# Attention with a gated MLP on one core: the query products, the output projection and the quotients are put in other places

## The chip, the cores and the metric

The kernel runs on one core of a Trainium2 chip. The core has a matrix engine (TensorE, PE in the profile; its weight loads are PEld), a vector engine (VectorE, DVE), a scalar engine (ScalarE, ACT), GpSimd (POOL) and a queue processor (SyncE, SP) from which nearly all DMAs of this kernel are issued. Each engine takes its own instructions in order and waits for others by semaphores. [...] The metric is the device time of one launch in microseconds. The kernel before takes 1242.56 us (median of three runs, 1242.16 to 1243.12).

## The reference

With x of 2048 tokens by 512 and 32 heads of width 128 over 2048 cached keys and values, all bf16:

```python
xn = layernorm(x)
q = (xn @ wq) per head                          # 32 heads of 128
p = softmax(q @ k_cache^T * 128**-0.5)          # 2048 x 2048 per head
s = concat_heads(p @ v_cache) @ wo              # 2048 x 512
h = gelu(layernorm(xn) @ w1)                    # four quarters, shifted by +1, -1, +2, -2 tokens
x1 = xn + shifted(h) @ w2
b = x1 + gelu(layernorm(x1) @ w3) @ w4          # w3: 512 x 1792
out = x + s * silu(b)
```

Nearly all of the work is the attention: scores, exponentials and weighted values for 32 heads.

## The kernel before, in words

The first 130 us or so compute the two normalisations and most of the MLP. Then comes one long loop over attention **units**. A unit is one head and one block of 512 query tokens: 8 groups of 4 heads, 4 query blocks per group, 4 heads, in that order, so 128 units, and four units in a row share their query block and head group. A unit has 8 **slots**, and a slot handles 256 keys: two score matmuls of 512 columns into a PSUM tile of two banks (`ps_s`, two such tiles), one exponential on ACT over 128x1024 into a bf16 tile (`pT`), and, ten slots later, two matmuls of these weights with the values (`ps_o`). The order of all instructions is written out by hand, slot by slot: each engine's program is the order in which the loop emits. Into the slots go further pieces, from here on called **extras** where they are TensorE's:

- **Query products.** The queries of two heads are made together by a seven-product scheme from xn (`xnT`, sums of it in `xs`) and the query weights (`wq_h`, sums and differences in `wc`), each product being two matmuls of 256 columns. For the pair with first unit v the products are spread over units v-2 (even) and v-1 (odd). Products 1, 6 and 2 are in the even unit, 7, 5, 4 and 3 in the odd one. They share one PSUM bank, tag `xa`: products 1 and 7 take a new tile of it. `q_take` (line 393, ACT) copies product 1 out (`tq`), and later the sum of products 1 and 2 (`qT`). `q_part` (lines 400 to 409, DVE) makes the other sums; its last step, line 407, frees the bank for the next pair.
- **Output projection.** When the four heads of a query block and group are done, four token tiles of 128 tokens are each multiplied with the four heads' `wo` rows: four matmuls of 512 columns per tile, one per chosen slot (`wo_slot`, list `at_wo`), into one PSUM bank (tag `xm`). The fifth step, `wo_post`, adds the tile's result to its fp32 sum (line 560, DVE). One tile is done per unit. In the last groups `wo_post` also plans scalings (lines 526 and 531) at slots counted from its own.
- **Softmax denominators.** DVE adds up the exponentials of a unit (lines 429, 434, 438, 442); a transposing DMA (`tT`) turns the result; DVE reduces it (`sm`, line 472) and takes the reciprocal (line 478). Through DRAM the reciprocals are written (`dr`) and read back as a broadcast to all partitions (`rb`). Two units later, in slot 7, `norm` (line 496, DVE) multiplies the unit's value result with `rb` into `oT`, the left side of the projection. Because of the transposing DMA, `rb` holds the tokens of the block in the order (p j), token j*128 + p. Before the change `oT` holds that order too, and the projection picks every fourth column.

DVE's program around the end of a unit reads: an addition of exponentials (slot 6), the projection's sum and the quotient (slot 7), the reduction, the reciprocal and another addition (slot 0 of the next unit). Units 14 to 123 follow the pattern that the change touches.

Of the kernel before, what the change touches and what calls it, by code (L numbers as in the profile page):

```python
# [17 lines left out]
def kernel(  # L18
# [26 lines left out]
    QT = Sq // 512  # L45
# [5 lines left out]
    HG = 4  # L51
# [77 lines left out]
    TURN = range(NU - HG)  # L129
# [185 lines left out]
    def q_mm(u, dcs, tag="xa"):  # L315
        g, qt, hh = units[u]
        if dcs[0] == 0:
            st[u] = dict(psq=psX.tile([P, 512], FP32, tag=tag, name="ps_q"))
        for dc in dcs:
            mm(st[u]["psq"][:], wqs[g * HG + hh][:, dc, :],  # L320
               xnT[:, dc, qt * 512:(qt + 1) * 512], dc == 0, dc == DC - 1)
# [73 lines left out]
    def q_part(v, i):  # L395
        s = sw[v]
        ps, t = s["ps"], lambda: pS.tile([P, 256], FP32, tag="tq", bufs=3, name="tq")
        if i == 0:
            s["u"] = t()
            pin(nc.vector.tensor_tensor(out=s["u"][:], in0=ps[:, 1, :], in1=s["m1"][:], op=ALU.add))  # L400
        elif i == 1:
            s["u3"] = t()
            pin(nc.vector.tensor_tensor(out=s["u3"][:], in0=ps[:, 0, :], in1=s["u"][:], op=ALU.add))
        elif i == 2:
            pin(nc.vector.tensor_tensor(out=s["q"][:, 3, :], in0=ps[:, 1, :], in1=s["u3"][:], op=ALU.add))
        else:
            pin(nc.vector.tensor_tensor(  # L407
                out=s["q"][:, 1:3, :], in0=ps[:], in1=s["u"][:].unsqueeze(1).to_broadcast([P, 2, 256]),
                op=ALU.add))
            del sw[v]  # L410

    def s_slot(u, p):
        g, qt, hh = units[u]
        s = st[u]
        sps = psS.tile([P, 2, 512], FP32, name="ps_s")
        for j in range(2):
            kc = 2 * p + j
            kv = kTs[g * HG + hh].rearrange("d (i p j) -> d i j p", p=P, j=KJ)
            mm(sps[:, j, :], kv[:, kc // KJ, kc % KJ, :], s["qT"][:], True, True)
        if p % 2 == 0:  # L420
            s.setdefault("pT", []).append(pB.tile([P, 4, 512], BF16, tag="pT", bufs=6, name="pT"))
        jj = 2 * (p % 2)
        pin(nc.scalar.activation(  # L423
            out=s["pT"][-1][:, jj:jj + 2, :], in_=sps[:], func=ACT.Exp, scale=SCALE))
# [7 lines left out]
    def add_next(u, i):  # L432
        a = st[u]["acc"]
        pin(nc.vector.tensor_tensor(out=a[:], in0=a[:], in1=st[u]["pT"][i][:], op=ALU.add))  # L434
# [34 lines left out]
    def turned_sums(u):  # L469
        s = st[u]  # L470
        sm = s["sm"] = smp.tile([P, 4], FP32, name="sm")
        pin(nc.vector.tensor_reduce(out=sm[:], in_=s["tT"][:], axis=mybir.AxisListType.X, op=ALU.add))  # L472

    def turned_recip(u):
        s = st[u]
        sm = s["sm"]
        rc = smp.tile([P, 4], FP32, name="rc")
        pin(nc.vector.reciprocal(out=rc[:], in_=sm[:]))
        s["dr"] = drp.tile([P, 4], FP32, name="dr")
        pin(nc.sync.dma_start(out=s["dr"][:], in_=rc[:]))  # L480

    def bcast(u):
        st[u]["rb"] = pB.tile([P, 512], FP32, tag="rb", bufs=2, name="rb")
        pin(nc.sync.dma_start(
            out=st[u]["rb"][:], in_=st[u]["dr"][:].rearrange("p j -> (p j)").partition_broadcast(P)))

    def norm(u):
        g, qt, hh = units[u]
        s = st.pop(u)
        if hh == 0:  # L490
            oTs[(g, qt)] = pB.tile([P, HG, 512], BF16, tag="oT", bufs=2, name="oT")
        o, rb, to = s["o"][:], s["rb"][:], oTs[(g, qt)][:, hh, :]
        if u in TURN:
            o = o.rearrange("k (j p) -> k p j", j=4)
            rb, to = (x.rearrange("k (p j) -> k p j", j=4) for x in (rb, to))
        pin(nc.vector.tensor_tensor(out=to, in0=o, in1=rb, op=ALU.mult))  # L496

    wo_box = {}
# [5 lines left out]

    def o_cols(g, qt, hh, ts):
        o = oTs[(g, qt)][:, hh, :]
        if (g * QT + qt) * HG + hh in TURN:
            return o.rearrange("k (p j) -> k j p", j=4)[:, ts, :]
        return o[:, ts * P:(ts + 1) * P]

    def wo_mm(g, t, hhs, tag="xm"):
# [28 lines left out]
    def pay():  # L540
        while owed:
            y_out(*owed.popleft(), nc.sync)
# [317 lines left out]
    def pv_run(n):  # L860
        while pv_at[0] <= n - LAG:
            pv_slot(*divmod(pv_at[0], SPU))
            pv_at[0] += 1
# [11 lines left out]
    def wo_slot(part, n, each=2, **kw):  # L875
        gg, t = wo_todo[0]
        if part < HG // each:
            wo_mm(gg, t, tuple(range(part * each, (part + 1) * each)), **kw)
            return
        wo_todo.popleft()  # L880
        wo_post(gg, t, n)
        if gg == NG - 1 and t % 4 < 3 and t + 1 not in fin and t // 4 not in LATE:
            fin_load(t + 1)
# [5 lines left out]
    first, third = {}, {}  # L889
    for v in pairs:  # L890
        a = (v - 2) * SPU
        for k, n in ((1, 1), (6, 2), (2, 5), (7, 8), (5, 9), (4, 12), (3, 13)):
            steps[a + n].append((product, v, k))
        for i, n in enumerate((1, 5)):
            steps[a + n].append((q_take, v, i))
        steps[a + 14].append((q_part, v, 3))
        first[v - 2] = v
        third[v - 1] = (v,)

    def fold_at(u):  # L900
        return 1 if u in third else 0

    def run_steps(n, which):
        for fn, v, k in steps.get(n, ()):
            if fn is which:
                fn(v, k)
# [4 lines left out]
    for h in range(HG, H, 2):  # L911
        u = (h // HG) * QT * HG + (-4, -2)[h % HG // 2]
# [8 lines left out]
    for n in range(UB * SPU):  # L921
        u, p = divmod(n, SPU)
        extra = len(wo_todo) > 1 and u in (2 * HG, 2 * HG + 1)
        if p == 0 and wo_box:
            wo_slot(4, n, each=1)
        s_slot(u, p)
        pv_run(n)
        for v, dcs in q_plan.get(n, ()):
            q_mm(v, dcs)
        run_steps(n, product)  # L930
        run_steps(n, q_take)
        if p == 0 and 1 <= u:
            if u - 2 in TURN:
                turned_sums(u - 2)
                turned_recip(u - 2)
            add_next(u - 1, 3)
        if p == 1 and u - 2 in TURN:
            bcast(u - 2)
        if p == fold_at(u) and 1 <= u:
            for v in third.get(u, ()):  # L940
                q_part(v, 1)
            fold(u - 1)
            for v in third.get(u, ()):
                q_part(v, 2)
            if u != UA and u not in first:
                fold_last(u - 1)
        if p == 2 and u in first:
            q_part(first[u], 0)
            fold_last(u - 1)
        if p == 3 and u - 1 in TURN:  # L950
            turn(u - 1)
        if p == 0:
            twice = extra
        if twice and p < 3:
            wo_slot(p, n, tag="xa")
        for v, k in ((u + 1, 3), (u + 2, 7)):
            if p == k and "psq" in st.get(v, ()) and (k == 3) == (v > FIRST):
                q_copy(v)
        if u - 2 in TURN:
            norm_p, sum_p, wo_p, each = 7, 5, 3, 1  # L960
        else:
            norm_p, sum_p, wo_p, each = 4, 5, 4, 1
        at_wo = [wo_p + i for i in range(HG // each + 1)]
        if FIRST - 2 <= u < LAST:
            at_wo = ([0, 3, 4, 6, 7], [0, 2, 3, 6, 7], [3, 4, 5, 6, 7], [0, 2, 3, 6, 7])[u % 4]
        if p == norm_p and 2 <= u and not u - 2 in TURN:
            norm_queue(u - 2)
        if p == sum_p and 1 <= u and u - 1 not in TURN:
            sums(u - 1)
        if p == sum_p + 1 and 1 <= u and u - 1 not in TURN:  # L970
            bcast(u - 1)
        if u == UA and p in (1, 2, 3):
            wo_slot(p - 1, n)
            if p == 3:
                fold_last(u - 1)
        if p in at_wo and wo_todo and pS is not None and (p == at_wo[0] or wo_box):
            wo_slot(at_wo.index(p), n, each=each)
        if p == norm_p and u - 2 in TURN:
            norm_queue(u - 2)
        run_steps(n, q_part)  # L980
        if p == 4:
            add_first(u)
        if p == 6:
            add_next(u, 2)
        pay()
        held_mm(n)
        for fn in todo.pop(n, ()):
            fn()
        if pS is None and not held:
            right.close()  # L990
            pS = right.enter_context(pool("pS", side="right", reuse_waits="tile"))
# [3 lines left out]
    n = UB * SPU  # L995
# [156 lines left out]
```

## Time and profile before

| | |
|---|---|
| median of three runs | 1242.56 us |
| profiled execution | 1240.9 us, its span 1239.1 us |
| TensorE, share of the span busy | 100% |
| ACT | 90% |
| DVE | 83% |
| DMA queue 1, share of 16 engines | 41.1% |
| granted TensorE clock | 1.0 |

The trace is of one execution. Engines' records give start, duration, line and the tiles written and read. Nearly every matmul is recorded under line 112, a helper, so matmuls are told apart by their tiles: `ps_s<-qT,kT` are scores, `ps_o<-pT,vb` weighted values, `ps_q` the query products, `ps_wo<-wo_h,oT` the output projection. Matmuls are pipelined and their ends are modelled, so a duration of 0.38 us for one of 512 columns is longer than the time from one start to the next. In the timeline, a row's first number is its start in microseconds from the start of the span, the second its duration, or that of the merged row where x2 or more stands at its end. In the chain of waits, each row is a piece of the chain that ended last. In the rows of groups, busy time and mean duration in ns stand behind the first bar, idle time before the group's instructions behind the second.

### The profile page before, as it was taken

What the parts mean: (1) busy time and instruction counts of PE and PEld (TensorE: products, weight loads), DVE (VectorE), ACT (ScalarE), POOL (GpSimd) and SP (SyncE); (2) the same over time, 40 slices, a digit from 0 to 9 for tenths busy, and PEclk for the clock granted to TensorE, in tenths of its full rate; (3) what the DMA queues carried; (4) which work ended last, traced back from release to release, by engine and by line L of the source; (5) the groups of instructions that cost most, each with busy time, mean ns of one, the idle gap of its engine ahead of it and who ended that gap; (6) DMA issues with size and microseconds to landing.
All of it is one profiled execution on the core that took longest, in us unless ns stands there. A gap on an engine that the chain in (4) does not pass through costs nothing.

```text
span 1239.1 us, 17537 instructions
## 1 busy us (share of the span) xinstructions
PE 1233.0 (100%) x6267; PEld 644.2 (52%) x6267; DVE 1030.3 (83%) x1647; ACT 1112.6 (90%) x1237; POOL 26.7 (2%) x75
## 2 busy tenths in 40 slices
PE   9999999999999999999999999999999999999998
PEld 6444444455555555555555555555555555555555
DVE  7712778898888888888889888888889999999997
ACT  6345999899999999999999999999999999999996
POOL 5300000000000000000000000000000000000000
PEclk9999999999999999999999999999999999999999
DMA  8760112554334423353243423443345435543332
GB/s 175 171 148 21 31 39 65 98 97 91 66 76 100 109 53 82 86 112 84 57 90 95 111 55 69 100 103 75 71 87 107 102 65 86 103 103 69 77 80 67
DMA packets 244056, 107.75 MB, mean 87 GB/s; under 512 B 194816, under 2 KB 227712, under 8 KB 243968
## 3 DMA queue, kind: packets, MB, share of 16 engines
q1 hardware_dynamic: 243408, 106.17, 41.1%
q8 instruction: 49, 0.80, 0.3%
q14 instruction: 39, 0.32, 0.1%
q10 hardware_dynamic: 560, 0.46, 0.1%
HBM read 67.50 MB, written 2.36 MB: 56 GB/s over the span
## 4 chain that ended last, share of the span: by engine, by line
PE 95%; DVE 3%; DMA 1%; ACT 1%; issue 0%; POOL 0%; DVEq 0%; ACTq 0%
PE ps_s L112 39%; PE ps_o L112 37%; PE ps_q L112 8%; PE ps_wo L112 8%; PE ps_m L112 2%; DVE acc L434 1%; ACT pT L423 1%; DMA rb<-dr 0%; DMA tT<-acc 0%; DVE sm L472 0%; DVE oT L496 0%; DMA xin<-in_A_x_dram 0%; PE ps_oh L112 0%; DMA dr<-rc 0%; DVE y L1014 0%
## 5 line engine op out<-in xcount | busy, mean ns | idle before, releaser
L423 ACT ACTIVATE pT<-ps_s 128x1024 bf16<-128x1024 f32 x1016 | 1019.8, 1025 | 54.4 <-PE ps_s L112 24.8
L112 PE MATMUL ps_s<-qT,kT 128*128 128x512 bf16 (+1 forms) x2064 | 609.0, 377 | 0.0
L112 PE MATMUL ps_o<-pT,vb 128*128 128x512 bf16 x1984 | 589.9, 379 | 0.0
L434 DVE TENSOR_TENSOR acc<-acc,pT 128x2048 bf16<-128x2048 bf16 x254 | 307.0, 1209 | 54.6 <-ACT pT L423 54.1
L112 PEld LDWEIGHTS <-kT 128*128 128x128 bf16 x2064 | 232.7, 113 | 147.4 <-issue 2.4
L112 PEld LDWEIGHTS <-vb 128*128 128x128 bf16 x1984 | 194.0, 98 | 216.9 <-issue 0.3
L429 DVE TENSOR_TENSOR acc<-pT 128x2048 bf16<-128x2048 bf16 x127 | 155.4, 1224 | 43.0 <-ACT pT L423 41.9
L112 PE MATMUL ps_wo<-wo_h,oT 128*128 128x512 bf16 x496 | 186.2, 379 | 0.0
L438 DVE TENSOR_TENSOR acc<-acc 128x1024 bf16<-128x1024 bf16 x127 | 87.4, 688 | 2.5
L496 DVE TENSOR_TENSOR oT<-ps_o,rb 128x512 bf16<-128x512 f32 x127 | 86.6, 682 | 1.5 <-DMA rb<-dr 1.2
L472 DVE TENSOR_REDUCE sm<-tT 128x4 f32<-128x512 bf16 x124 | 83.9, 677 | 2.0 <-DMA tT<-acc 2.0
L112 PEld LDWEIGHTS <-oT 128*128 128x128 bf16 x528 | 59.1, 112 | 49.5 <-issue 0.6
L112 PEld LDWEIGHTS <-wc 128*128 128x128 bf16 x440 | 42.9, 98 | 57.9 <-issue 12.7
L560 DVE TENSOR_TENSOR sacc<-ps_wo,sacc 128x512 f32<-128x512 f32 x96 | 65.7, 684 | 0.0
L112 PEld LDWEIGHTS <-wq_h 128*128 128x128 bf16 x398 | 38.9, 98 | 46.3
L112 PE MATMUL ps_q<-xnT,wq_h 128*128 128x256 bf16 (+1 forms) x288 | 61.1, 298 | 0.4 <-DVE sacc L548 0.4
L407 DVE TENSOR_TENSOR qT<-ps_q,tq 128x512 bf16<-128x512 f32 x55 | 38.0, 692 | 23.7 <-PE ps_q L112 23.5
L442 DVE TENSOR_TENSOR acc<-acc 128x512 bf16<-128x512 bf16 x127 | 53.0, 417 | 0.5
L293 ACT ACTIVATE h2T<-ps_s 128x1024 bf16<-128x1024 f32 x28 | 28.7, 1024 | 25.9 <-PE ps_s L112 25.9
L112 PEld LDWEIGHTS <-w_sb 128*128 128x128 bf16 x368 | 33.6, 98 | 29.6
L112 PE MATMUL ps_s<-xn2T,w_sb 128*128 128x512 bf16 x224 | 48.8, 379 | 0.0
L112 PE MATMUL ps_q<-xs,wc 128*128 128x256 bf16 x246 | 46.8, 271 | 0.0
(102 smaller groups left out, 586.4 us busy)
## 6 DMA issues: line engine op xcount, KB each, us to landing
rb<-dr SPq DMA_DIRECT2D x127, 256.0 KB, 3.9
vb<-in_A_v_cache_dram SPq DMA_DIRECT2D x62, 256.0 KB, 3.0
wq_h<-in_A_wq_dram SPq DMA_DIRECT2D x32, 128.0 KB, 3.1
wo_h<-in_A_wo_dram SPq DMA_DIRECT2D x32, 128.0 KB, 2.7
w_sb<-in_B_w_dram SPq DMA_DIRECT2D x8, 256.0 KB, 5.1
kT<-in_A_k_cache_dram SPq DMA_TRANSPOSE x128, 2.8
xl<-in_A_x_dram SPq DMA_DIRECT2D x16, 128.0 KB, 3.0
dr<-rc SPq DMA_DIRECT2D x127, 2.0 KB, 1.4
```

Of the source, the lines that this page charges most:

```text
L112: pin(nc.tensor.matmul(out=out, lhsT=lhsT, rhs=rhs, start=start, stop=stop, **kw))
L293: pin(nc.scalar.activation(out=h2[c, f][:], in_=ps[:], func=ACT.Gelu_apprx_tanh))
L407: pin(nc.vector.tensor_tensor(out=s["q"][:, 1:3, :], in0=ps[:], in1=s["u"][:].unsqueeze(1).to_broadcast([P, 2, 256]), op=ALU.add))
L423: pin(nc.scalar.activation(out=s["pT"][-1][:, jj:jj + 2, :], in_=sps[:], func=ACT.Exp, scale=SCALE))
L429: pin(nc.vector.tensor_tensor(out=s["acc"][:], in0=s["pT"][0][:], in1=s["pT"][1][:], op=ALU.add))
L434: pin(nc.vector.tensor_tensor(out=a[:], in0=a[:], in1=st[u]["pT"][i][:], op=ALU.add))
L438: pin(nc.vector.tensor_tensor(out=a[:, 0:2, :], in0=a[:, 0:2, :], in1=a[:, 2:4, :], op=ALU.add))
L442: pin(nc.vector.tensor_tensor(out=a[:, 0, :], in0=a[:, 0, :], in1=a[:, 1, :], op=ALU.add))
L472: pin(nc.vector.tensor_reduce(out=sm[:], in_=s["tT"][:], axis=mybir.AxisListType.X, op=ALU.add))
L496: pin(nc.vector.tensor_tensor(out=to, in0=o, in1=rb, op=ALU.mult))
L560: pin(nc.vector.tensor_tensor(out=sa, in0=ps[:], in1=sa, op=ALU.add))
```

## The change

- Product 1 of a query pair goes from slot 1 to slot 0 of its even unit, and so does the ACT copy of it.
- The four projection matmuls of a unit go to slots 3, 4, 6 and 7 of even units and 2, 3, 6 and 7 of odd ones. Before, the lists were 0, 3, 4, 6 (u%4 = 0), 0, 2, 3, 6 (odd) and 3, 4, 5, 6 (u%4 = 2), with the sum in slot 7.
- The lists have four entries now instead of five, so the sum is emitted by the rule at the top of the loop, `if p == 0 and wo_box`, at the head of the next unit, ahead of its first score matmuls. On DVE it so comes behind the quotient that slot 7 emits.
- The quotient (`norm`) walks the tokens in their own order: it reads PSUM and writes `oT` contiguously and reads `rb` at every fourth value. `o_cols` then picks 128 adjacent columns.

```diff
         if u in TURN:
-            o = o.rearrange("k (j p) -> k p j", j=4)
-            rb, to = (x.rearrange("k (p j) -> k p j", j=4) for x in (rb, to))
+            o, to = (x.rearrange("k (j p) -> k j p", j=4) for x in (o, to))
+            rb = rb.rearrange("k (p j) -> k j p", j=4)
         pin(nc.vector.tensor_tensor(out=to, in0=o, in1=rb, op=ALU.mult))
...
     def o_cols(g, qt, hh, ts):
         o = oTs[(g, qt)][:, hh, :]
-        if (g * QT + qt) * HG + hh in TURN:
-            return o.rearrange("k (p j) -> k j p", j=4)[:, ts, :]
         return o[:, ts * P:(ts + 1) * P]
...
-        for k, n in ((1, 1), (6, 2), (2, 5), (7, 8), (5, 9), (4, 12), (3, 13)):
+        for k, n in ((1, 0), (6, 2), (2, 5), (7, 8), (5, 9), (4, 12), (3, 13)):
             steps[a + n].append((product, v, k))
-        for i, n in enumerate((1, 5)):
+        for i, n in enumerate((0, 5)):
             steps[a + n].append((q_take, v, i))
...
         if FIRST - 2 <= u < LAST:
-            at_wo = ([0, 3, 4, 6, 7], [0, 2, 3, 6, 7], [3, 4, 5, 6, 7], [0, 2, 3, 6, 7])[u % 4]
+            at_wo = ([3, 4, 6, 7], [2, 3, 6, 7])[u % 2]
```

## The prediction

> **What bounds the kernel now.** I read the page first (busy time, chain of waits), then the chain in order of time, the busy time by stage and the row of one line, then the timeline of two places, last the groups and the waits. From the page:
>
> ```profile
> PE 1233.0 (100%) x6267; PEld 644.2 (52%) x6267; DVE 1030.3 (83%) x1647; ACT 1112.6 (90%) x1237; POOL 26.7 (2%) x75
> ...
> PE 95%; DVE 3%; DMA 1%; ACT 1%; issue 0%; POOL 0%; DVEq 0%; ACTq 0%
> ```
>
> TensorE carries 95% of the chain. A busy share of 100% doesn't say that it runs at its pace, so I compare pace with need. One row of the chain gives the pace, the row of line 393 (the copy of product 1, one per query pair) the real time, and the stage between its first and last start the busy times (PE, PEld, DVE, ACT, POOL, clock):
>
> ```profile
> 69.80 12.09 PE ps_o L112 x56
> ```
>
> ```profile
> L393 ACT ACTIVATE tq<-ps_q x55: 377/402/416, 249.1 to 1177.4; 128x256 f32<-128x256 f32 x55
> ```
>
> ```profile
> 249.10:1177.40 928.30, 927.65 (x4645) 486.44 (x4644) 821.18 (x1286) 888.24 (x974) 0.00 (x0) 1.00 0.42 86
> ```
>
> 56 matmuls of 512 columns take 12.09 us, 0.2159 us each. 54 pairs take 928.3 us, 17.19 each. A pair needs 2 x 16 score and 2 x 16 value matmuls, 8 of the output projection, and 7 products, each two matmuls of 256 columns, which I count as one of 512: 79 x 0.2159 = 17.06 us. The difference is 0.13 us, over 54 pairs 7 us. That is all that a better order of the same matmuls can win in this stage. The clock is 1.00. DVE idles 928.3 - 821.2 = 107 us, 0.99 us per unit (108 units), which is the cover for anything that DVE does more.
>
> Where the 0.13 us goes is seen at the slot after product 1. First a unit with u%4 = 0, TensorE and then ACT:
>
> ```profile
> 609.23 0.38 PE L112 MATMUL ps_q<-xnT,wq_h 128*128 128x256 bf16 x2
> 609.45 0.59 PE L112 MATMUL ps_s<-qT,kT 128*128 128x512 bf16 x2
> 609.88 0.59 PE L112 MATMUL ps_o<-pT,vb 128*128 128x512 bf16 x2
> 610.35 0.27 PE L112 MATMUL ps_q<-xs,wc 128*128 128x256 bf16 x1
> ```
>
> ```profile
> 609.92 0.38 ACT L393 ACTIVATE tq<-ps_q 128x256 f32<-128x256 f32 x1
> 610.18 1.03 ACT L423 ACTIVATE pT<-ps_s 128x1024 bf16<-128x1024 f32 x1
> ```
>
> Then one with u%4 = 2:
>
> ```profile
> 624.39 0.59 PE L112 MATMUL ps_s<-qT,kT 128*128 128x512 bf16 x2
> 624.82 0.59 PE L112 MATMUL ps_o<-pT,vb 128*128 128x512 bf16 x2
> 625.25 0.59 PE L112 MATMUL ps_s<-qT,kT 128*128 128x512 bf16 x2
> 625.68 0.59 PE L112 MATMUL ps_o<-pT,vb 128*128 128x512 bf16 x2
> 626.12 0.38 PE L112 MATMUL ps_q<-xnT,wq_h 128*128 128x256 bf16 x2
> 626.33 0.59 PE L112 MATMUL ps_s<-qT,kT 128*128 128x512 bf16 x2
> 626.76 0.59 PE L112 MATMUL ps_o<-pT,vb 128*128 128x512 bf16 x2
> 627.34 0.38 PE L112 MATMUL ps_q<-xs,wc 128*128 128x256 bf16 x2
> ```
>
> ```profile
> 624.16 2.86 ACT L423 ACTIVATE pT<-ps_s 128x1024 bf16<-128x1024 f32 x3
> 626.89 0.40 ACT L393 ACTIVATE tq<-ps_q 128x256 f32<-128x256 f32 x1
> ```
>
> Product 6 (ps_q from xs and wc) should start 2 x 0.216 us after the value matmuls: at 610.31 and 627.19. It starts at 610.35 and 627.34, 0.04 and 0.15 us late. Both times that is 0.05 us after the copy has ended (609.92 + 0.38 = 610.30; 626.89 + 0.40 = 627.29): product 6 writes the bank that the copy reads, and waits for it. The second place is worse because slot 0 there holds no extra matmul: the score matmuls of slots 0 and 1 come 0.86 us apart (624.39, 625.25). ACT needs more: three exponentials in 2.86 us, the last 1.03 us long, are a start every 0.92 us. ACT falls behind and takes the copy later.
>
> **The change, part by part.** The sum stands against the profiled execution (1240.9 us with what lies around its span); the median of the runs, 1242.56, is 1.7 us higher, and I take the same difference off it.
>
> *Product 1 and its copy one slot earlier.* Nothing is added; two matmuls and one copy move. On the first place's clock, slot 0 then has product 1 at 609.23 and the copy done at 610.30, as slot 1 has now. Slot 1 is left without an extra. Product 6 follows 0.22 (product 1) + 2 x 0.86 us (slot 1, and slot 2's score and value matmuls) after 609.23: 611.17, which is 0.82 us after the bank is free. The stall goes: the mean of 0.04 and 0.15 times 55 pairs, 5.2 us, under the ceiling of 7. What is late next: the exponential of slot 1 starts behind the copy at 610.18 and ends at 611.21; with 0.05 us of release its bank is free at 611.26, and the score matmuls of slot 3 want it at 611.17 + 0.22 = 611.39. The cover is 0.13 us: cost 0, but thin (a rival). Product 1 must also wait for the last addition of the pair before (line 407), which frees the bank. DVE, and TensorE's product 4:
>
> ```profile
> 619.60 0.42 DVE L405 TENSOR_TENSOR qT<-ps_q,tq 128x256 bf16<-128x256 f32 x1
> ...
> 622.65 0.69 DVE L407 TENSOR_TENSOR qT<-ps_q,tq 128x512 bf16<-128x512 f32 x1 [0.53 <-PE ps_q L112]
> 623.25 1.22 DVE L434 TENSOR_TENSOR acc<-acc,pT 128x2048 bf16<-128x2048 bf16 x1
> 624.39 0.68 DVE L560 TENSOR_TENSOR sacc<-ps_wo,sacc 128x512 f32<-128x512 f32 x1
> 624.99 0.68 DVE L496 TENSOR_TENSOR oT<-ps_o,rb 128x512 bf16<-128x512 f32 x1
> ```
>
> ```profile
> 621.15 0.38 PE L112 MATMUL ps_q<-xnT,wc 128*128 128x256 bf16 x2
> ```
>
> Line 407 ends at 623.34; product 1 would come 0.86 us into the slot that starts at 624.39, at 625.25: 1.9 us of cover, cost 0. For the first pair, line 327's query copy of slot 111 frees the bank; it stands on DVE where line 560 stands here, ends near 625.07 on this clock and is covered too, once.
>
> *The output projection in fixed slots.* Four matmuls per unit as before. Even units now have one extra in slots 0 and 2 to 7, odd units one in each; before, slot 7 was empty, odd slot 0 and one even slot 5 double. TensorE's sum is the same. The gain is counted already: with slots 7 and 0 filled ACT isn't behind when product 1 comes.
>
> *Sums at the unit's head.* The sum (line 560) changes place with the quotient (line 496) on DVE: the quotient at 624.39, the sum at 624.99. The matmul that it adds starts 0.86 us into slot 7, which began 0.86 us before 624.39, so at about 624.39, and ends 0.38 us later: no wait, and the reduction and reciprocal behind both keep their time. The bank is free at 625.67; the next tile's first matmul comes two slots and 0.86 us after 624.39, near 627.4. The quotient asks for its broadcast 0.6 us sooner; what it waits, DVE's idle time takes. Cost 0.
>
> *Scaling in the late groups.* Line 526 is queued from the sum's slot. In odd units it falls behind line 405, no longer ahead of it. Chain, then waits:
>
> ```profile
> 963.13 0.60 DVE sacc L526
> ...
> 965.05 0.38 PE ps_q L112 x2
> ```
>
> ```profile
> PE ps_q L112 <- DVE qT L405: 0.6, 2, 0.4
> ```
>
> At 965.05 the chain passes from DVE into product 4, with this 0.60 us in it. Out of the way, it ends these two waits, 0.6 us in all if the second is alike: gain 0.6.
>
> *Quotients in token order.* The operation reads PSUM contiguously instead of every 128th value, the broadcast at every 4th fp32 instead of contiguously, and writes contiguously as before; the projection's weight load, with a step until now, becomes contiguous.
>
> ```profile
> L112 PEld LDWEIGHTS <-kT 128*128 128x128 bf16 x2064 | 232.7, 113 | 147.4 <-issue 2.4
> L112 PEld LDWEIGHTS <-vb 128*128 128x128 bf16 x1984 | 194.0, 98 | 216.9 <-issue 0.3
> ...
> L496 DVE TENSOR_TENSOR oT<-ps_o,rb 128x512 bf16<-128x512 f32 x127 | 86.6, 682 | 1.5 <-DMA rb<-dr 1.2 <-PE ps_o L112 0.3
> ...
> L560 DVE TENSOR_TENSOR sacc<-ps_wo,sacc 128x512 f32<-128x512 f32 x96 | 65.7, 684 | 0.0
> ```
>
> A weight load with a step (kT) takes 113 ns, one without (vb) 98; either ends inside the 216 ns of the matmul before: gain 0. The quotient: a step in PSUM costs nothing (682 against 684 ns for the contiguous sum). No DVE row reads SBUF with a step; the nearest row is that weight load, 15% dearer, which would make 0.78 us. Bounds: 0.67 us (a gain too small to matter) to twice the 0.60 us between 624.39 and 624.99, 1.20. I take 0.68, the same engine's row. Up to about 0.9 us more would cost TensorE nothing: DVE has 0.99 us idle per unit, and product 4 at 621.15 stands 1.13 us behind the end of line 405 (620.02).
>
> [...]
>
> The sum: -5.2 - 0.6 = -5.8 us, from 1242.56 to 1236.8 (profiled: 1240.9 to 1235.1).
>
> **Rivals.** (1) The exponential takes product 6's place as the wait: if the 0.13 us of cover is overdrawn by 0.05 to 0.1 us, each of 55 pairs loses that, 2.8 to 5.5 us, and the kernel ends at 1239.6 to 1242.3. For it: ACT is busy 888.24 of 928.30 us. Against: it can start every 0.92 us, in slots of 1.08. (2) The quotient doubles to 1.20 us. DVE spends 0.6 of its 0.99 us; late broadcasts then reach TensorE now and then, and I allow up to half of the gain: 1237 to 1240, still faster. (3) The slower side: the read with a step takes so long that DVE becomes the bound. This decides from about 1.6 us per quotient (0.60 + 0.99); at three times the price, 1.8 us, DVE lacks 0.2 us in 108 units, 22 us, and the end is near 1259. For it: no row prices this read. Against: the step of 512 bytes in PSUM is free. (4) The change doesn't do what it says: product 6 waits for something that moves with it. Then 1242. Against: it starts 0.05 us after the copy's end in both places.
>
> **How the numbers follow.** A measurement of this kernel tells 0.2% (2.5 us) from no change. Forecast 0.58 and rival 2 0.14 are faster; rival 1 0.08 and rival 4 0.04 within; rival 3, to which I add what else may delay DVE, 0.16. So faster 0.72, same 0.12, slower 0.16. The range starts at 1235.0, where nearly all of the 7 us and the 0.6 are won, and ends at 1242.0, which leaves out little but rival 3. The forecast's own range is 1235.0 to 1239.0.
>
> **What would show it.** Right: the copies of product 1 near 17.08 us per pair apart instead of 17.19; product 6 directly behind the value matmuls; TensorE's wait for line 405 gone; line 496 near 680 ns, the oT weight load near 98. Wrong: line 496 above 1.2 us with TensorE waiting for DVE, score matmuls late in slot 3 of even units, or pairs still 17.19 us apart.

## The result: 1.6% slower, and the profile after

The changed kernel takes 1261.44 us (median of four runs, 1260.29 to 1265.34) against 1242.36 us for the kernel before beside it. The ratio is 1.016, 95% interval 1.0136 to 1.0183. I had forecast 1236.8. The profiled execution took 1260.29 us, its span 1258.5.

The page of the changed kernel: busy time, the chain of waits by engine and by line, two groups.

```profile
PE 1233.7 (98%) x6267; PEld 636.8 (51%) x6267; DVE 1077.8 (86%) x1647; ACT 1112.1 (88%) x1237; POOL 26.6 (2%) x75
...
PE 60%; DVE 19%; DMA 18%; issue 1%; ACT 1%; SPq 1%; DVEq 0%; ACTq 0%
PE ps_s L112 25%; PE ps_o L112 23%; DMA rb<-dr 10%; DMA dr<-rc 5%; PE ps_q L112 5%; PE ps_wo L112 5%; DVE oT L496 4%; DVE acc L434 4%; DMA tT<-acc 2%; DVE sm L472 2%; PE ps_m L112 2%; DVE sacc L558 2%; DVE acc L429 1%; DVE acc L438 1%; ACT pT L423 1%
...
L496 DVE TENSOR_TENSOR oT<-ps_o,rb 128x512 bf16<-128x512 f32 x127 | 135.5, 1067 | 33.1 <-DMA rb<-dr 31.4
...
L112 PEld LDWEIGHTS <-oT 128*128 128x128 bf16 x528 | 51.4, 98 | 59.1 <-issue 1.3
```

TensorE's busy time is the same, but it carries 60% of the chain instead of 95%. In its place stand DVE and two DMAs, the reciprocals' way out to DRAM (`dr<-rc`) and back as a broadcast (`rb<-dr`). The quotient of line 496 takes 1.07 us instead of 0.68. The list of waits of the changed kernel (total us, times, longest):

```profile
DVE oT L496 <- DMA rb<-dr: 31.4, 50, 2.4
...
PE ps_q L112 <- DVE qT L405: 17.3, 18, 2.1
```

50 quotients now wait for their broadcast, where 2 did, and TensorE waits 17.3 us for line 405, where it waited 0.6. (The projection's sum, line 560 before, has line 558 here.)

What the change does to product 6 came as forecast. TensorE's timeline of the changed kernel, product 1 in slot 0 and product 6 in slot 2:

```profile
611.56 0.38 PE L112 MATMUL ps_q<-xnT,wq_h 128*128 128x256 bf16 x2
...
613.07 0.59 PE L112 MATMUL ps_o<-pT,vb 128*128 128x512 bf16 x2
613.50 0.38 PE L112 MATMUL ps_q<-xs,wc 128*128 128x256 bf16 x2
613.72 0.59 PE L112 MATMUL ps_s<-qT,kT 128*128 128x512 bf16 x2
```

Product 6 starts 0.43 us, two matmuls, after the value matmuls, without the 0.04 or 0.15 us of delay. Yet the copies of product 1 are further apart:

```profile
L393 ACT ACTIVATE tq<-ps_q x55: 377/381/390, 248.8 to 1191.0; 128x256 f32<-128x256 f32 x55
```

942.2 us for 54 pairs is 17.45 us per pair, against 17.19 before: 13.9 us lost in this stage. Another 5.8 us lie behind it: from the last copy to the end of the span 67.5 us, 61.7 before.

The loss isn't spread evenly. By the starts of the single copies, 36 of the 54 pairs take 17.06 or 17.07 us in the changed kernel, the need of the prediction. The first 46 pairs together take 792.5 us against 790.3 before, the last eight 149.7 against 138.0. So of the 19.4 us by which the span grows, 17.5 fall into the last eight pairs and what follows them. From here on the **late groups** are the projections of the last group and of half the one before: there the sum is two operations (lines 551 and 554), or further ones come behind it (lines 567 and 569). One stretch there, before and then after (busy times of PE, PEld, DVE, ACT, POOL with the instructions, clock, DMA share, GB/s):

```profile
1060.00:1170.00 110.00, 109.60 (x550) 57.51 (x549) 102.91 (x163) 104.77 (x116) 0.00 (x0) 1.00 0.44 89
```

```profile
1060.00:1170.00 110.00, 101.72 (x508) 52.20 (x506) 100.19 (x153) 96.69 (x106) 0.00 (x0) 1.00 0.47 84
```

TensorE starts 508 matmuls there instead of 550, and DVE, although its quotients are dearer, is busy less than before. A DVE that is short of time doesn't look like that.

**Where the time went.** DVE around a unit's head in the changed kernel, in a part that runs without a stall:

```profile
610.48 1.08 DVE L496 TENSOR_TENSOR oT<-ps_o,rb 128x512 bf16<-128x512 f32 x1
611.48 0.68 DVE L558 TENSOR_TENSOR sacc<-ps_wo,sacc 128x512 f32<-128x512 f32 x1
612.08 0.67 DVE L472 TENSOR_REDUCE sm<-tT 128x4 f32<-128x512 bf16 x1
612.78 0.18 DVE L478 RECIPROCAL rc<-sm 128x4 f32<-128x4 f32 x1
```

From the quotient's start to the next reciprocal's start it is 2.30 us. Before, it was 1.30 (624.99 to 626.29). Now the same stretch in the chain of waits, in the late groups:

```profile
1076.35 1.00 DVE oT L496
...
1141.30 1.09 DVE oT L496
1142.38 0.61 DVE tm L551
...
1143.02 0.69 DVE sacc L554
1143.71 0.61 DVE sm L472
...
1144.34 0.19 DVE rc L478
...
1144.54 2.86 DMA dr<-rc
...
1147.42 3.28 DMA rb<-dr
...
1150.72 1.07 DVE oT L496
...
1159.98 1.08 DVE oT L496
```

This chain closes: the reciprocal starts the DMAs, the broadcast releases the quotient, and because DVE works in order (before the quotient at 1141.30 it sits idle for 1.10 us, until the broadcast has landed), the next unit's reduction and reciprocal stand behind that quotient. One turn per unit. The turn shown takes 9.42 us (1141.30 to 1150.72), the nine from 1076.35 to 1159.98 take 9.29 on average, and TensorE's unit is half of 17.06, 8.53. So in the late groups the units run at the pace of this chain, and DVE's additions and line 405, which product 4 waits for, come late.

That the chain is near its limit could be seen in the kernel before. Its timeline at a unit's head, and two rows of the DMA issues (the last number is the median time to landing):

```profile
626.29 0.18 DVE L478 RECIPROCAL rc<-sm 128x4 f32<-128x4 f32 x1
...
626.50 0.34 SPq L480 DMA_DIRECT2D dr<-rc  x1
...
628.94 0.34 SPq L484 DMA_DIRECT2D rb<-dr  x1
```

```profile
rb<-dr SPq DMA_DIRECT2D x127, 256.0 KB, 3.9
...
dr<-rc SPq DMA_DIRECT2D x127, 2.0 KB, 1.4
```

2.65 us from the reciprocal to the broadcast's issue, 3.9 to its landing, 1.30 on DVE: 7.85 us, 0.7 below 8.53. The change adds 0.4 (quotient) and 0.6 (the sum, now between quotient and reduction), which makes 8.85. But the way out varies: 2.44 us here, 2.86 in the chain above, 1.4 in the median. With the median a turn is about 1.0 us shorter, some 6.8 before and 7.8 after, and fits. In the late groups the sum is two operations, so 0.7 more, and there a turn no longer fits: of the nine above, eight are longer than 8.53. In the changed kernel the broadcast also lands later, 4.3 us in the median instead of 3.9; the runs don't show why.

### The profile page after: what moved, and what is told of

Same layout as the page of the kernel before. It is cut to its first block, busy times and chain, and to the rows that moved or that the text cites. A ratio compares the mean times of both kernels' runs of the same rounds, so it can differ in the third digit from the quotient of the medians.

```text
span 1258.5 us, 17538 instructions
## 1 busy us (share of the span) xinstructions
PE 1233.7 (98%) x6267; PEld 636.8 (51%) x6267; DVE 1077.8 (86%) x1647; ACT 1112.1 (88%) x1237; POOL 26.6 (2%) x75
## 4 chain that ended last, share of the span: by engine, by line
PE 60%; DVE 19%; DMA 18%; issue 1%; ACT 1%; SPq 1%; DVEq 0%; ACTq 0%
PE ps_s L112 25%; PE ps_o L112 23%; DMA rb<-dr 10%; DMA dr<-rc 5%; PE ps_q L112 5%; PE ps_wo L112 5%; DVE oT L496 4%; DVE acc L434 4%; DMA tT<-acc 2%; DVE sm L472 2%; PE ps_m L112 2%; DVE sacc L558 2%; DVE acc L429 1%; DVE acc L438 1%; ACT pT L423 1%
## 5 line engine op out<-in xcount | busy, mean ns | idle before, releaser
L496 DVE TENSOR_TENSOR oT<-ps_o,rb 128x512 bf16<-128x512 f32 x127 | 135.5, 1067 | 33.1 <-DMA rb<-dr 31.4
L112 PEld LDWEIGHTS <-oT 128*128 128x128 bf16 x528 | 51.4, 98 | 59.1 <-issue 1.3
L112 PE MATMUL ps_q<-xnT,wc 128*128 128x256 bf16 x194 | 37.0, 272 | 17.4 <-DVE qT L405 17.3
```

Of the source, the lines that this page charges most:

```text
L112: pin(nc.tensor.matmul(out=out, lhsT=lhsT, rhs=rhs, start=start, stop=stop, **kw))
```

## The experiments

The times are medians, each with the kernel before on the same chip and the ratio's 95% interval. The three theories are named in the first expectation: the chain (there called loop), DVE's load (occupancy), the sum's place as such.

**The quotient as before** (`e1_old_quotient`): the changed kernel with both edits of the quotient undone.

```diff
-            o, to = (x.rearrange("k (j p) -> k j p", j=4) for x in (o, to))
-            rb = rb.rearrange("k (p j) -> k j p", j=4)
+            o = o.rearrange("k (j p) -> k p j", j=4)
+            rb, to = (x.rearrange("k (p j) -> k p j", j=4) for x in (rb, to))
...
+        if (g * QT + qt) * HG + hh in TURN:
+            return o.rearrange("k (p j) -> k j p", j=4)[:, ts, :]
```

> The changed kernel with the quotient in its old order (PSUM read with a step, broadcast contiguous) and the old column picking; slots, product 1 and the sum's place stay changed. Three theories. Loop: the chain reciprocal, DMA out, DMA back, quotient, what stands on DVE up to the next reciprocal closes once per unit and must fit into TensorE's 8.53 us; in the changed kernel DVE's part of it is 2.31 us (3.04 to 3.50 in the late groups) against 1.31 before. Here it falls by 0.4 to 1.91, still 0.6 above before: most stalls go, some in the late groups stay; 1237 to 1244 us. Occupancy: only the 0.4 us more DVE work per quotient matters: all of the loss goes, 1236 to 1238 us. Place: the sum at the unit's head is what hurts: about 1258 to 1261 us.

1240.86 us, before 1240.58: ratio 1.0001 (0.9992 to 1.0011). With 0.39 us less per quotient the 1.6% are gone, but of what the slots should gain nothing is left over. That is inside the chain's range and above the one of occupancy.

**The quotient alone** (`e2_quotient_only`): the kernel before with the same two edits the other way round.

> The kernel before with only the quotient in token order; everything else as before. Loop: DVE's part grows from 1.31 to 1.71 us, in the late groups too, since the sum stands ahead of the quotient; product 6 still waits for the copy: 1242 to 1248 us. Occupancy: the whole of the extra DVE work is here, so at least the loss of the changed kernel: 1261 us or more. Place: nothing moves: 1242 us. In any case line 496 takes about 1.08 us and the oT weight load 98 ns.

1246.89 us, before 1240.58: 1.0049 (1.0034 to 1.0064).

```profile
L496 DVE TENSOR_TENSOR oT<-ps_o,rb 128x512 bf16<-128x512 f32 x127 | 134.9, 1062 | 3.5 <-DMA rb<-dr 3.1
```

The same dear quotient, the same extra DVE work as in the changed kernel, and 6 us of loss instead of 19. Occupancy as I had put it can't give that; neither is it nothing. On this run's page DVE is busy 90% or more in every slice from 1060 to 1170 us, so how much of the 6 us is the longer chain and how much is DVE's load stays open.

**The sum behind the next reciprocal** (`e3_sum_behind_recip`): the changed kernel, same operations, one of them later in DVE's order.

```diff
-        if p == 0 and wo_box:
+        if p == 0 and wo_box and not FIRST - 2 < u <= LAST:
             wo_slot(4, n, each=1)
...
                 turned_recip(u - 2)
+            if wo_box and FIRST - 2 < u <= LAST:
+                wo_slot(4, n, each=1)
```

> The changed kernel with the projection's sum emitted behind the next reciprocal instead of behind the quotient; the same operations of the same length on DVE, so the same DVE work. Loop: DVE's part of it falls from 2.31 to about 1.71 us and is no longer longer in the late groups; 1236 to 1241 us. Occupancy: same work, so no change: 1260 us. Place: the sum is still at the unit's head, 0.8 us later: 1260 us or more.

1241.71 us, before 1240.58: 1.0008 (0.9999 to 1.0017). With the same DVE work, 1.5% come back by taking 0.6 us (1.3 in late groups) out of the closed chain. That decides against occupancy and against the sum's place at the head as such. The time lies 0.7 us above the range that I had given for the chain.

**Both** (`e4_old_quotient_sum_behind`): the edits of the first and the third.

> Both: the old quotient and the sum behind the reciprocal; slots and product 1 as in the changed kernel. Loop: DVE's part is 1.31 us as before the change, and the gain that the slots should bring is left alone: 1236 to 1238 us, pairs 17.08 us apart. Occupancy: the same as e1_old_quotient. Place: about 1260 us.

1236.84 us, before 1240.58: 0.9971 (0.996 to 0.9982). Its rows: the spacing of the copies, and three waits.

```profile
L393 ACT ACTIVATE tq<-ps_q x55: 378/381/392, 248.5 to 1172.8; 128x256 f32<-128x256 f32 x55
```

```profile
DVE sm L472 <- DMA tT<-acc: 4.2, 7, 1.1
DVE oT L496 <- DMA rb<-dr: 2.3, 4, 1.2
...
PE ps_q L112 <- DVE qT L405: 1.5, 4, 0.9
```

17.12 us per pair, against 17.06 of need: the slots and product 1 do bring most of what they should, 3.7 us of the 5.8 forecast, once the chain has its old length. Beside this kernel the dear quotient costs 0.4% (e3), the sum between quotient and reduction 0.3% (e1), and both together 1.9%: the parts don't add up. That fits a chain that costs only what it exceeds TensorE's unit by. What the dear quotient costs alone may be DVE's load instead: in `e3` DVE is busy 106.45 of the 110 us from 1060 to 1170.

**Quotient and sum behind the reciprocal**, token order kept (`e5_quotient_behind_recip`) and with the old quotient (`e6_old_quotient_behind_recip`). To `e3` comes, for units 14 to 123:

```diff
                 turned_recip(u - 2)
+            if FIRST - 2 < u <= LAST:
+                norm_queue(u - 3)
...
-        if p == norm_p and u - 2 in TURN:
+        if p == norm_p and u - 2 in TURN and not FIRST - 2 <= u < LAST:
             norm_queue(u - 2)
```

> The changed kernel, token order kept, with the quotient of unit u-2 and the projection's sum both emitted behind the next unit's reciprocal. DVE does the same operations of the same length. Loop: the next reciprocal no longer stands behind the quotient, so a late broadcast can't delay it within one unit; the chain closes only over two units and has 17 us. 1236 to 1239 us, the wait of the quotient for its broadcast nearly gone, although the quotient still takes 1.08 us. Occupancy: 1260 us as the changed kernel.

> The same with the old quotient of 0.68 us. Loop: open and with 0.4 us less DVE work ahead of line 405; at or below e4_old_quotient_sum_behind, 1235 to 1237 us. Occupancy: 1236 to 1238 us, with all the difference to e5 (24 us) from the quotient's length.

1250.91 us, 1.0085 (1.007 to 1.01), and 1239.95 us, 0.9995 (0.9985 to 1.0004), before 1240.82. Both lie outside what either theory gave. Row and wait of the first:

```profile
L496 DVE TENSOR_TENSOR oT<-ps_o,rb 128x512 bf16<-128x512 f32 x127 | 132.5, 1043 | 0.3 <-PE ps_o L112 0.3
```

```profile
DVE sm L472 <- DMA tT<-acc: 18.9, 23, 1.9
```

The wait for the broadcast is gone, as the open chain wants it. But the reduction now waits 18.9 us for the transposing DMA (2.4 in the changed kernel, 4.2 in e4); with the old quotient, in `e6`, it waits 12.8. That DMA stands behind the last fold (line 442), the fold behind the additions, these behind the reciprocal: a second chain that closes once per unit, and quotient and sum had been put into it. How much of the loss is this chain and how much the dense DVE of the late groups, these runs don't separate.

**The step on the write** (`e7_step_on_write`): `e3` with the quotient in token order, the broadcast read contiguously and `oT` written with a step.

```diff
-            o, to = (x.rearrange("k (j p) -> k j p", j=4) for x in (o, to))
-            rb = rb.rearrange("k (p j) -> k j p", j=4)
+            o, to = (x.rearrange("k (j p) -> k p j", j=4) for x in (o, to))
+            rb = rb.rearrange("k (p j) -> k p j", j=4)
```

> e3_sum_behind_recip with the quotient in token order by a step on its write: it reads PSUM with a step as before, the broadcast contiguously, and writes every 128th bf16 of oT, 256 bytes apart. If the 0.4 us belongs to reading SBUF with a step alone, line 496 takes 0.68 us and the time is that of e4_old_quotient_sum_behind, 1236 to 1238 us, with the oT weight load at 98 ns. If any step in SBUF costs, about 1.08 us and 1241 us, as e3.

1311.98 us, 1.0575 (1.056 to 1.0591). Neither of the two cases: the write with a step is far dearer than the read.

```profile
L496 DVE TENSOR_TENSOR oT<-ps_o,rb 128x512 bf16<-128x512 f32 x127 | 304.9, 2401 | 7.1 <-DMA rb<-dr 6.4
```

```profile
DVE 62%; PE 20%; DMA 9%; issue 6%; ACT 1%; DVEq 0%; SPq 0%; ACTq 0%
```

At 2.4 us per quotient, 1.7 more than the old one, DVE carries 62% of the chain of waits and is busy 91% of the span. Here DVE itself may be the bound, as my third rival had it; but the closed chain is longer by the same 1.7 us, and this run doesn't separate the two.

**The chain made longer with no work added** (`e9_late_broadcast`): `e4` with the broadcast issued behind the transposing DMA.

```diff
-        if p == 1 and u - 2 in TURN:
+        if p == 1 and u - 2 in TURN and not 16 <= u < LAST:
             bcast(u - 2)
...
             turn(u - 1)
+            if 16 <= u < LAST:
+                bcast(u - 2)
```

> e4_old_quotient_sum_behind with the broadcast of units 16 to 123 issued behind the transposing DMA on the DMA queue instead of ahead of it. No engine does more; the issue comes about 4.15 us behind the reciprocal instead of 1.6 to 3, so the chain is 4.15 + 3.9 to 4.3 + 1.31 = 9.4 to 9.8 us per unit against TensorE's 8.53. Loop: 0.9 to 1.2 us more in each of 108 units, 1332 to 1367 us. Occupancy: no change, 1237 us.

1378.72 us (one run, no interval), 142 us over `e4`, and above the range that I gave. Its busy times and its chain of waits:

```profile
PE 1265.5 (92%) x6267; PEld 645.1 (47%) x6267; DVE 1029.9 (75%) x1647; ACT 1117.6 (81%) x1237; POOL 26.6 (2%) x75
```

```profile
603.15 0.69 DVE oT L496
...
604.47 0.18 DVE rc L478
...
609.26 3.85 DMA rb<-dr
...
613.13 0.69 DVE oT L496
```

A turn is 9.98 us, and DVE does nothing more: it is busy 1029.9 us, 1030.5 in `e4`. It isn't quite the same chain: in the rows left out behind the reciprocal it now runs through the sum, DVE's additions and folds and the issue of the transposing DMA, and the broadcast comes behind them. But a chain that is too long costs the time here with no work added.

**The price of a step** (`e8_price_of_step`): at the end of `e4` four operations each of these kinds, their results thrown away.

```diff
+    def by(x, s):
+        return x if s == 1 else x.rearrange("k (p j) -> k j p", j=s)
...
+            pin(nc.vector.tensor_tensor(out=like(dd[:], 4), in0=like(pp[:], 4), in1=by(f32, 4), op=ALU.mult))
```

> e4_old_quotient_sum_behind with 56 more operations on DVE behind the last store, their results thrown away: products of a 128x512 fp32 PSUM tile with fp32 or bf16 of SBUF into bf16, four of each, with one side read or written at steps of 1, 2, 4, 8 or 16 elements. From the runs so far: 0.68 us at step 1, 1.08 for fp32 in SBUF at step 4 (16 bytes), 0.68 for PSUM at any step, about 2.4 for a write far apart. [...] The whole run is some 45 us longer.

1290.43 us (one run), 53.6 over `e4`, where I had expected some 45; what counts here are the single operations. The groups: lines 1138, 1143, 1148, 1153 and 1158 read fp32 of SBUF (`sacc`) at steps of 1, 2, 4, 8 and 16 elements; 1163 and 1168 fp32 of PSUM (`pp`, which a matmul wrote) at 4 and 16; 1183 and 1188 bf16 of SBUF (`xall`) at 4 and 8; 1198 and 1203 write bf16 (`dd`) at 4 and 16.

```profile
L1203 DVE TENSOR_TENSOR dd<-pp,sacc 128x512 bf16<-128x512 f32 x4 | 9.2, 2299 | 0.1
L1198 DVE TENSOR_TENSOR dd<-pp,sacc 128x512 bf16<-128x512 f32 x4 | 5.2, 1294 | 0.1
L1153 DVE TENSOR_TENSOR dd<-pp,sacc 128x512 bf16<-128x512 f32 x4 | 4.3, 1066 | 0.1
...
L1188 DVE TENSOR_TENSOR dd<-pp,xall 128x512 bf16<-128x512 f32 x4 | 4.2, 1048 | 0.1
L1148 DVE TENSOR_TENSOR dd<-pp,sacc 128x512 bf16<-128x512 f32 x4 | 4.2, 1046 | 0.1
L1158 DVE TENSOR_TENSOR dd<-pp,sacc 128x512 bf16<-128x512 f32 x4 | 4.0, 1004 | 0.1
L1143 DVE TENSOR_TENSOR dd<-pp,sacc 128x512 bf16<-128x512 f32 x4 | 2.8, 691 | 0.1
L1163 DVE TENSOR_TENSOR dd<-pp,sacc 128x512 bf16<-128x512 f32 x4 | 2.8, 691 | 0.1
L1168 DVE TENSOR_TENSOR dd<-pp,sacc 128x512 bf16<-128x512 f32 x4 | 2.8, 691 | 0.1
...
L1183 DVE TENSOR_TENSOR dd<-pp,xall 128x512 bf16<-128x512 f32 x4 | 2.8, 691 | 0.1
L1138 DVE TENSOR_TENSOR dd<-pp,sacc 128x512 bf16<-128x512 f32 x4 | 2.8, 689 | 0.1
```

A read of SBUF at a step of 8 bytes is free (fp32 at 2, bf16 at 4: 0.69 us), at 16 bytes it costs 0.36 us more (fp32 at 4, bf16 at 8: 1.05), and two and four times that step cost about the same (1.07 and 1.00). A read of PSUM at a step of 16 or 64 bytes is free (0.69). A write of bf16 with a step costs 0.6 us more at 8 bytes and 1.6 at 32.

**The sum ahead of the quotient** (`e10_sum_ahead`): the kernel before with product 1 and its copy in slot 0 and slots that keep clear of it.

```diff
-        for k, n in ((1, 1), (6, 2), (2, 5), (7, 8), (5, 9), (4, 12), (3, 13)):
+        for k, n in ((1, 0), (6, 2), (2, 5), (7, 8), (5, 9), (4, 12), (3, 13)):
...
-        for i, n in enumerate((1, 5)):
+        for i, n in enumerate((0, 5)):
...
-            at_wo = ([0, 3, 4, 6, 7], [0, 2, 3, 6, 7], [3, 4, 5, 6, 7], [0, 2, 3, 6, 7])[u % 4]
+            at_wo = ([1, 3, 4, 6, 7], [0, 2, 3, 6, 7])[u % 2]
```

> The kernel before with product 1 and its copy in slot 0, and one change of the projection's slots: even units take 1, 3, 4 and 6, odd ones 0, 2, 3 and 6 as before; the sum stays in slot 7 ahead of the quotient, the quotient is the old one. There are two chains that close once per unit: reciprocal, DMA out and back, quotient, reduction, reciprocal (what stands on DVE from the quotient to the reciprocal lengthens it), and transposing DMA, reduction, reciprocal, additions and folds, transposing DMA (what stands on DVE from the reduction to the last fold lengthens it). Ahead of the quotient the sum lies in neither. Two chains: product 6's wait goes and no new wait comes, 1234.5 to 1236.5 us, 0.3 to 0.5% below before and below e4_old_quotient_sum_behind. If instead filling slot 7 is what removes the stall of product 6, half of it stays and the time is 1238 to 1239 us.

1236.12 us, before 1240.95: 0.9962 (0.9948 to 0.9975), the lowest time of all and ahead of both kernels; from `e4` (0.9971) it isn't clear of the noise.

```profile
PE 94%; DVE 3%; DMA 1%; ACT 1%; issue 1%; SPq 0%; DVEq 0%; ACTq 0%
```

```profile
L393 ACT ACTIVATE tq<-ps_q x55: 392/392/405, 248.3 to 1171.7; 128x256 f32<-128x256 f32 x55
```

17.10 us per pair, and TensorE carries the chain again. Slot 7 is empty in every unit here, so filling it isn't what removes the stall of product 6; moving product 1, with the even units' slots kept clear of it, is.

## Why the prediction was wrong, point by point

- **Pace, need and the stall of product 6: right.** 17.06 us of need per pair is what the changed kernel reaches in 36 of 54 pairs, and product 6 starts on time. `e10_sum_ahead` keeps this part, with other slots for the even units, and gains 4.8 us; I had put it at 5.2.
- **Cover of the moved product and the slots: right.** Product 1 doesn't wait for line 407, and the score matmuls after product 6 are on time (613.72), so rival 1 fell.
- **"Sums at the unit's head ... Cost 0": the step that failed, and the same yardstick for the quotient with it.** I looked at what the sum waits for and at the order of the rest, and found no wait. I didn't follow what it stands in front of: between the quotient and the reduction it lengthens by 0.6 us, 1.3 in the late groups, the chain that goes through two DMAs and closes once per unit. "What it waits, DVE's idle time takes" was the wrong yardstick. Idle time before the additions is of no use to a chain that waits for a landing; e3, with the same work in another order, shows it (1241.71 us against 1261.44). Put at nothing, the sum costs 4.0 us alone (e1 against e4) and, with the dear quotient beside it, 1.5% (the changed kernel against e3): turns of 9.29 us on average where TensorE's unit is 8.53.
- **The quotient: 0.68 us taken, 1.07 measured.** It lay inside the bounds of 0.67 to 1.20. I went by the free step in PSUM and the 15% of the weight load, and e8 shows that neither is a measure for a read of SBUF in steps of 16 bytes: 1.05 us there, 0.69 at 8 bytes. The upper bound, a doubling, was my estimate; no row of the kernel before prices such a read. That up to about 0.9 us more "would cost TensorE nothing" failed too: alone, the 0.39 us cost 6 us (e2) or 4.9 (e3 against e4), by the chain or by DVE's load in the late groups.
- **Rival 2** named what did cost time, broadcasts so late that TensorE feels it, but priced it at half of the gain at most, 1237 to 1240 us, by DVE's average idle time; without the sum in the chain the dear quotient takes the whole gain (e3, 1241.71). **Rival 3** named the right side with the wrong mechanism: a DVE that has no time left, from 1.6 us per quotient on. DVE is busy 86% of the span here, and e3 has the same work at 1241.7.
- **Line 526 behind line 405, 0.6 us: not shown.** The wait of TensorE for line 405, 0.6 us before, is 17.3 us in the changed kernel and 1.5 in e4, so this gain appears in neither. I didn't try this part alone.
- **The weight load of `oT`: right**, 98 ns. That it gains nothing wasn't tried alone; no run shows a gain from it.

## What to carry to other kernels

Where an engine works in order and a DMA's answer comes back into its own queue, look for chains that close once per iteration, add up every operation and landing in them, and compare the sum with the iteration; average idle time says nothing about that margin. An operation that nothing waits for soon belongs where no such chain passes: here that is the stretch from the last fold to the quotient, where e10 has the sum (1236.12 us). Price a change of an access pattern on the side that gets the step, and by its bytes (here, in e8, 0.69 us for a read of SBUF at 8 bytes and 1.05 at 16, 1.29 for a write at 8 and 2.30 at 32).

## What the runs showed of the hardware that I had not expected

- In products of fp32 in PSUM with SBUF into bf16 (one run, e8), DVE took 0.69 us per 512 values with SBUF read at steps of up to 8 bytes and 1.00 to 1.07 at steps of 16 to 64 bytes; with PSUM read at steps of 16 and 64 bytes it took 0.69. Writes of bf16 with a step were dearer: 1.29 us at 8 bytes, 2.30 at 32, 2.4 at 256 (e7).
- Two delays of 0.4 and 0.6 us that cost 0.4% and 0.3% one at a time cost 1.9% together.
